# Scaling attention's value result instead of its exponentials in the first six blocks

## The chip, the cores and the metric

The kernel runs on one core of one Trainium2 chip. The metric is device time of one execution in microseconds (us). Before the change the median of three runs was 721.8 us (721.43 to 722.63). A change of less than about 0.2% (1.4 us) cannot be told from none.

## What is computed

Two stages, both in float32, with inputs `q`, `k`, `v` of 4 batches, 8 heads, 768 positions and 64 values per head:

```python
scores = scale * np.matmul(q, k.transpose(0, 1, 3, 2)) + bias      # bias: -slope of the head * distance
scores = np.where(keep, scores, -1e9)                              # 96 positions back, and the first 8
a = np.exp(scores - np.max(scores, axis=-1, keepdims=True))
a = a / (np.sum(a, axis=-1, keepdims=True) + 1e-09)
attn_out = np.matmul(a, v)
x = attn_out.transpose(0, 2, 1, 3).reshape(B * S, H * D)           # 3072 x 512
h = x @ w_in                                                       # 512 x 2048
out = (h * (1.0 / (1.0 + np.exp(-h)))) @ w_out                     # 2048 x 512
```

The weights `w_in` and `w_out` arrive as 64-bit floats, so the kernel first makes float32 of them.

## The kernel before, in words

Attention works in 24 blocks of 128 positions (4 batches of 6), all 8 heads at once, in four pairs of heads (`hp`). For a head, a block's 128 rows of queries meet a window of 232 keys (96 before the block, 8 global ones, the block's own 128); the first block of a batch has 128 keys alone. For each pair:

- TensorE makes the scores (`scores`, L532, for blocks 0 to 5; `stack_scores`, L508, from block 6 on).
- VectorE adds the bias and takes the row's extreme in one instruction (`top_of`, L542), and ScalarE makes the exponentials and their row sums (`expo`, L550).
- VectorE adds 1e-9 to the sums (`guard`, L557), inverts them (`inverse`, L561) and multiplies the exponentials by them, one instruction for each head (`norm`, L566).
- TensorE transposes the scaled exponentials with an identity (`turn_p`, L580), ScalarE copies them out of PSUM (`move_p`, L594).

Then `values_of` (L608) makes the block's result `av` in one bank of PSUM, transposed: its rows are a pair's 2 x 64 values, its columns the 128 positions, for four pairs side by side. ScalarE rounds it to the high part `xh` (L620), and VectorE takes the rest as the low part `xl` (L623).

The second stage works in 12 groups of two blocks (256 positions). For each of 16 chunks `f` of the 2048 inner values: 12 matmuls of L726 (the three products high*high, low*high, high*low of a split float32, 4 row chunks), tanh and the gate (L732 to L744), 6 matmuls of L751 into the group's output banks.

Weights are 32 transfers of 512 KB (`stage`, L364), `w_in` chunk and `w_out` chunk in turn. VectorE makes float32 of a pair of words in three steps (L368, L374, L380), ScalarE rounds it to the high part (L387), VectorE takes the low part (L391). The landing places are three tiles of a pool with the tag "big", and, in turn for two of every five of the first 20 transfers, two places that are filled with weights of their own only at the end ("lent", `wl`).

The order of all this is made beforehand: `Plan.run` walks through a list of operations with a cost, a rank, dependencies and the buffers that they hold, and for every engine takes the lowest rank among the ready ones; the emitted program has that order on each engine, and each engine follows it strictly. While TensorE finds nothing in the first 60 us of the plan, the plan puts in a `filler`, a bf16 matmul on a tile of zeros (L862). Attention's operations have ranks by block and pair, the conversion of transfer `n` has rank 14 + n. So the pairs of blocks 0 to 3 go ahead of most of the conversion, and those of blocks 4 and 5 stand among it.

Of the kernel before, what the change touches and what calls it, by code (L numbers as in the profile page):

```python
# [170 lines left out]
def attn_moe(ctx, tc, q, k, v, n_global, n_local, w_in, w_out, out):  # L171
# [428 lines left out]
    def values(i, hp, av):  # L600
# [3 lines left out]
        for c in range(0 if i % NJ else 1, 2):  # L604
            for a in range(2):
# [5 lines left out]
                )  # L611

    def x_part(i, x):
        g, jj = divmod(i, NB)
# [4 lines left out]
    def x_high(i):
        nc.scalar.copy(x_part(i, "xh"), blk[i]["av"])  # L620

    def x_low(i):
        nc.vector.tensor_sub(x_part(i, "xl"), blk[i]["av"], x_part(i, "xh").bitcast(F32))  # L623
# [414 lines left out]
```

## Time and profile before

| | |
|---|---|
| median of three runs | 721.8 us |
| the profiled execution | 722.34 us |
| its span, first to last instruction | 720.5 us |
| granted TensorE clock, mean | 0.998 |
| busy share: TensorE, VectorE, ScalarE, GpSimd | 98%, 66%, 58%, 3% |

A page of the profile names the engines PE (TensorE matmul), PEld (its weight load), DVE (VectorE), ACT (ScalarE), POOL (GpSimd), SP (SyncE, which issues transfers). Matmuls are pipelined: the duration of one is longer than the step from its start to the next one's start, so a busy PE need not be at its peak. VectorE and ScalarE overlap the end of one instruction with the start of the next by about 0.08 to 0.1 us; in a row of instructions the step from start to start is what one costs. A float32 matmul that is not split stands as two records.

### The profile page before, as it was taken

The numbers are of one execution on the slowest core, as the hardware profiler recorded it, in microseconds if no ns is written. First come the engines' busy times: TensorE is split into PE (matmuls) and PEld (weight loads), VectorE is DVE, ScalarE is ACT, GpSimd is POOL, SyncE is SP. The second block draws the span as 40 slices with busy tenths as digits, with TensorE's granted clock in tenths as the row PEclk, the third lists the DMA queues.
The fourth block names the chain that finished last, engine by engine and source line by source line (L and its number), as shares of the span: only waits on it lengthen the run. The fifth ranks groups of instructions, "written<-read, shape, count | busy, mean of one in ns | idle before, by whom it ended". The sixth has DMA issues, their size and how long they took to land.

```text
span 720.5 us, 14013 instructions
## 1 busy us (share of the span) xinstructions
PE 709.5 (98%) x5144; PEld 630.3 (87%) x5144; DVE 476.1 (66%) x1489; ACT 419.9 (58%) x1097; POOL 24.9 (3%) x81
## 2 busy tenths in 40 slices
PE   8999999999999999999999999999999999999996
PEld 5778899888899999998999999999899999998995
DVE  5999999768756656666566666665665766543332
ACT  5977444579656657566566565665665756443321
POOL 2000000010000000000000000000000000000000
PEclk9999999999999999999999999999999999999999
DMA  8895546362404215124133142340421412000000
GB/s 155 207 246 170 167 126 178 84 173 74 115 12 133 65 51 144 45 71 114 37 97 99 47 116 65 81 112 10 126 73 42 130 30 56 30 2 1 30 1 34
DMA packets 117499, 63.95 MB, mean 89 GB/s; under 512 B 93744, under 2 KB 110384, under 8 KB 117424
## 3 DMA queue, kind: packets, MB, share of 16 engines
q1 hardware_dynamic: 116992, 62.86, 32.3%
q8 instruction: 42, 0.69, 0.4%
q14 instruction: 33, 0.27, 0.1%
q10 hardware_dynamic: 432, 0.13, 0.1%
HBM read 56.69 MB, written 6.29 MB: 87 GB/s over the span
## 4 chain that ended last, share of the span: by engine, by line
PE 92%; ACT 3%; DVE 2%; DMA 1%; issue 1%; SPq 0%; ACTq 0%; DVEq 0%
PE bank L726 36%; PE bank L751 35%; PE bank L608 6%; PE bank L580 5%; PE bank L508 4%; PE bank L448 3%; PE bank L532 2%; ACT pe L550 1%; PE bank L862 1%; DMA c<-in_moe_w_in_dram 1%; DMA qn<-in_q_dram 1%; ACT R L499 0%; DVE th L736 0%; ACT gh L740 0%; DVE pe L542 0%
## 5 line engine op out<-in xcount | busy, mean ns | idle before, releaser
L726 PE MATMUL bank<-xh,WIH 128*128 128x256 f32 x768 | 225.4, 293 | 0.0
L726 PE MATMUL bank<-xl,WIH 128*128 128x256 f32 x768 | 216.2, 281 | 0.0
L726 PE MATMUL bank<-xh,WIL 128*128 128x256 f32 x768 | 215.0, 280 | 0.0
L726 PEld LDWEIGHTS bank<-xh,WIH 128*128 128x128 f32 x768 | 144.7, 188 | 10.3 <-issue 3.3
L726 PEld LDWEIGHTS bank<-xl,WIH 128*128 128x128 f32 x768 | 144.7, 188 | 6.2
L726 PEld LDWEIGHTS bank<-xh,WIL 128*128 128x128 f32 x768 | 144.8, 189 | 0.0
L732 ACT ACTIVATE th<-bank 128x256 f32<-128x256 f32 x192 | 73.7, 384 | 106.1 <-PE bank L726 103.9
L751 PE MATMUL bank<-WOH,gh 128*128 128x512 f32 x336 | 135.2, 403 | 0.0
L751 PE MATMUL bank<-WOH,gl 128*128 128x512 f32 x336 | 132.5, 394 | 0.0
L751 PE MATMUL bank<-WOL,gh 128*128 128x512 f32 x336 | 132.1, 393 | 0.0
L740 ACT CAST gh<-th 128x256 fp32r<-128x256 f32 x192 | 77.2, 402 | 77.3 <-PE bank L751 50.5
L744 DVE TENSOR_TENSOR gl<-th,gh 128x256 fp32r<-128x256 f32 x192 | 81.4, 424 | 54.3 <-ACT gh L740 51.4
L736 DVE SCALAR_TENSOR_TENSOR th<-th,bank 128x256 f32<-128x256 f32 x192 | 80.2, 418 | 55.6 <-ACT th L732 53.5
L550 ACT ACTIVATE pe<-pe,NM 128x232 f32<-128x232 f32 (+1 forms) x192 | 90.7, 473 | 32.0 <-DVE NM L542 30.2
L542 DVE CUSTOM_DVE_ANT_0 pe<-bank,B 128x232 f32<-128x232 f32 (+1 forms) x192 | 68.7, 375 | 55.9 <-PE bank L508 53.0
L751 PEld LDWEIGHTS bank<-WOH,gl 128*128 128x128 f32 x336 | 63.0, 187 | 15.3
L751 PEld LDWEIGHTS bank<-WOH,gh 128*128 128x128 f32 x336 | 63.4, 189 | 7.2 <-issue 0.8
L751 PEld LDWEIGHTS bank<-WOL,gh 128*128 128x128 f32 x336 | 63.4, 189 | 6.8
L594 ACT COPY pt<-bank 128x512 f32<-128x512 f32 (+1 forms) x80 | 43.7, 548 | 28.7 <-PE bank L580 28.5
L566 DVE TENSOR_SCALAR pe<-pe,rs 128x232 f32<-128x232 f32 (+1 forms) x192 | 55.8, 328 | 1.5
L580 PE MATMUL bank<-ident,pe 128*128 128x128 f32 (+1 forms) x352 | 55.7, 275 | 1.1 <-DVE pe L566 1.0
L580 PEld LDWEIGHTS bank<-ident,pe 128*128 128x128 f32 (+1 forms) x352 | 41.4, 136 | 11.3 <-DVE pe L566 2.9
(117 smaller groups left out, 877.7 us busy)
## 6 DMA issues: line engine op xcount, KB each, us to landing
c<-in_moe_w_in_dram SPq DMA_DIRECT2D x16, 512.0 KB, 4.7
c<-in_moe_w_out_dram SPq DMA_DIRECT2D x16, 512.0 KB, 4.4
vn<-in_v_dram SPq DMA_DIRECT2D x24, 256.0 KB, 3.5
w<-in_moe_w_in_dram SPq DMA_DIRECT2D x12, 512.0 KB
w<-in_moe_w_out_dram SPq DMA_DIRECT2D x12, 512.0 KB, 3.7
kn<-in_k_dram SPq DMA_DIRECT2D x23, 256.0 KB, 3.1
qn<-in_q_dram SPq DMA_DIRECT2D x23, 256.0 KB, 3.1
out_dram<-osb SPq DMA_DIRECT2D x23, 256.0 KB, 3.1
```

Of the source, the lines that this page charges most:

```text
L542: nc.vector.tensor_tensor_reduce(t["p", hp][:, a, :n], t["s", hp][a][:, :n], B1[:, h] if i % NJ else B0[:, h], -SC, 3.0e38, ALU.add, ALU.m ...
L550: nc.scalar.activation(x, x, AF.Exp, bias=NM[:, i * H + h:i * H + h + 1], scale=-1.0, accum_out=t["sum", hp][:, a:a + 1],)
L566: nc.vector.tensor_scalar(x, x, t["inv", hp][:, a:a + 1], None, ALU.mult)
L580: nc.tensor.transpose(ps[:n, c, a], pe[:, a, c0:c0 + n], ident)
L594: nc.scalar.copy(t["pt", hp][:, c], t["tp", hp][:, c])
L608: nc.tensor.matmul(pav[r, hp], x[:, 2 * hp + a], pt[:P if c else C1, c, a], start=not c or not i % NJ, stop=c == 1,)
L726: nc.tensor.matmul(ph, w[:, c, fs], x[:, c], start=not c and not n, stop=c == NCC - 1 and n == 2)
L732: nc.scalar.activation(th, mo["ph", g, f], AF.Tanh, scale=0.5)
L736: nc.vector.scalar_tensor_tensor(gf, gf, 1.0, mo["ph", g, f], ALU.add, ALU.mult)
L740: nc.scalar.copy(gh, mo["th", g, f])
L744: nc.vector.tensor_sub(gl, mo["th", g, f], mo["gh", g, f].bitcast(F32))
L751: nc.tensor.matmul(po, a[:, s], w_o(w, f), start=f == 0 and n == 0, stop=f == NFC - 1 and n == 2)
```

## The change

In blocks 0 to 5 the exponentials stay unscaled. The row sums of a block's 8 heads go to one tile of 8 columns (`sums`). When the block's last exponentials are done, VectorE adds 1e-9 (`guard_all`), inverts (`inverse_all`), and writes the rounded inverses and what rounding left to columns 0 to 7 and 8 to 15 of a tile `inv` (`inverse_high`, `inverse_low`). TensorE turns that tile (`turn_inv`), ScalarE copies it out (`move_inv`), and four matmuls with a selecting matrix of zeros and ones (`spread_inv`) write to a bank, for each pair, the inverse sums in the layout of `av`: each of the 64 rows of a head holds that head's inverse of the position. ScalarE copies `av` to SBUF (`move_av`), VectorE multiplies it with the bank (`norm_all`), and `x_high` and `x_low` read the product from SBUF.

GpSimd makes the selecting matrix at the start (`sel`: two clears, 16 selects on 64 columns each, one copy). `inv`, the turned tile and the selecting matrix live in one of the three "big" tiles, held from the start until the last `spread_inv` of block 5. Blocks 6 to 23 are as before. The plan makes its order anew, with all of this in its list.

```diff
+            elif not hp:
+                t["sums"] = x = sb3.tile([P, H], F32, name="sums")
+                for y in range(NHP):
+                    t["sum", y] = x[:, 2 * y:2 * y + 2]
...
+    def sel():
+        nc.gpsimd.memset(st["sel0"], 0.0)
+        for hp in range(NHP):
+            for a in range(2):
+                for p in range(2):
+                    nc.gpsimd.affine_select(
+                        st["sel0"][:, hp, a * D:(a + 1) * D], st["sel0"][:, hp, a * D:(a + 1) * D],
+                        [[0, D]], ALU.not_equal, 1.0, base=-(2 * hp + a + p * H), channel_multiplier=1,
+                    )
+        nc.gpsimd.tensor_copy(st["sel"], st["sel0"])
+    def guard_all(i):
+        x = blk[i]["sums"]
+        nc.vector.tensor_scalar(x, x, 1e-9, None, ALU.add)
+    def inverse_all(i):
+        x = blk[i]["sums"]
+        nc.vector.reciprocal(x, x)
+    def inverse_high(i):
+        nc.vector.tensor_copy(st["inv"][:, :H], blk[i]["sums"])
+    def inverse_low(i):
+        nc.vector.tensor_sub(st["inv"][:, H:2 * H], blk[i]["sums"], st["inv"][:, :H].bitcast(F32))
+    def turn_inv(i, tp):
+        st["it", i] = ps = bank(tp, P)
+        nc.tensor.transpose(ps, st["inv"].bitcast(F32), ident)
+    def move_inv(i):
+        nc.scalar.copy(st["invt"], st["it", i])
+    def spread_inv(i, tp):
+        st["is", i] = ps = bank(tp, NHP, P)
+        for hp in range(NHP):
+            nc.tensor.matmul(ps[:, hp], st["sel"][:, hp], st["invt"], start=True, stop=True)
+    def move_av(i):
+        t = blk[i]
+        t["xq"] = x = sb2.tile([P, NHP, P], F32, name="xq", tag="mid", bufs=5)
+        nc.scalar.copy(x, t["av"])
+    def norm_all(i):
+        t = blk[i]
+        x = t["xq"]
+        nc.vector.tensor_mul(x, x, st["is", i])
+        t["av"] = x
...
+        x = sb3.tile([P, 8, P], F32R, name="inv", tag="big")
...
+    o_sel = op("POOL", 6000, -50, clear, [o_i], [ib, Buf("pt")])
...
-            o = op("DVE", 67, u - PAR["RI"], (lambda i=i, hp=hp: guard(i, hp)), o_e, [pe])
-            o = op("DVE", 72, u - PAR["RI"], (lambda i=i, hp=hp: inverse(i, hp)), [o], [pe])
-            o = [op("DVE", 250 if j else 196, u - PAR["RN"], (lambda i=i, hp=hp, a=a: norm(i, hp, a)), [o], [pe])
-                 for a in range(2)]
+            plain = i >= PAR["IV"]
+            o, o_all = o_e, o_all + o_e
+            if plain:
...
+        if not plain:
+            xq, tp, tq = Buf("pt"), Buf("tp"), Buf("tp")
...
+            m = op("ACT", 478, r, (lambda i=i: move_av(i)), [last], [pav, xq])
+            last = op("DVE", 602, r, (lambda i=i: norm_all(i)), [o, m], [tq, xq, xb[g]["xh"], xb[g]["xl"]])
+            pav = xq
```

How the order moves, at three places. First VectorE (DVE) around the end of block 0. `ISA pe,NM<-...` is `top_of`; before:

```order
L542 ISA pe,NM<-bank_87,B_91 128x128
L542 ISA NM 128x1
L566 TENSOR_SCALAR pe<-pe,rs 128x128 x2
L557 TENSOR_SCALAR rs<-sm 128x2
L542 ISA pe,NM<-bank_85,B_91 128x128
L542 ISA NM 128x1
L561 RECIPROCAL rs<-rs 128x2
L566 TENSOR_SCALAR pe<-pe,rs 128x128 x2
L542 ISA pe,NM<-bank_89,B_90 128x232
```

and now (lines of the new kernel: L547 is `top_of`, L636 to L646 the four steps on the sums, L668 `norm_all`):

```order
L636 TENSOR_SCALAR sums<-sums 128x8
L640 RECIPROCAL sums<-sums 128x8
L547 ISA pe,NM<-bank_87,B_90 128x232
L547 ISA NM 128x1
L643 CAST inv<-sums 128x8
L547 ISA pe,NM<-bank_85,B_90 128x232
L547 ISA NM 128x1
L646 TENSOR_TENSOR inv<-sums,inv 128x8
L547 ISA pe,NM<-bank_88,B_90 128x232
```

Two scalings, a guard and an inverse for each pair are gone; four steps on 8 columns stand once for the block, and `top_of` of the next block moves up between them. Over the program VectorE loses 40 scalings of 232 columns, 8 of 128, 24 guards and 24 inverses, and gains 6 times four small steps and one multiply of 512 columns.

Second, ScalarE (ACT) ahead of its first rounding of weights (L387 `CAST WIH`). Before:

```order
L594 COPY pt<-bank_85 128x512
L550 ACTIVATE pe,sm<-pe,NM 128x232
L511 COPY KHw<-bank_84 128x4x128
L550 ACTIVATE pe,sm<-pe,NM 128x232 x2
L511 COPY QHw<-bank_83 128x512
L550 ACTIVATE pe,sm<-pe,NM 128x232
L594 COPY pt<-bank_88 128x512
L550 ACTIVATE pe,sm<-pe,NM 128x232 x3
L387 CAST WIH<-wf_434 128x4x128
```

and now (L555 is `expo`, L599 `move_p`, L678 `x_high`):

```order
L599 COPY pt_q<-bank_83 128x512
L678 CAST xh<-xq 128x4x128
L555 ACTIVATE pe,sums<-pe,NM 128x232
L599 COPY pt_k<-bank_87 128x512
L555 ACTIVATE pe,sums<-pe,NM 128x232 x2
L599 COPY pt_k<-bank_85 128x512
L511 COPY KHw<-bank_89 128x4x128
L511 COPY QHw<-bank_88 128x512
L599 COPY pt<-bank_84 128x512
L555 ACTIVATE pe,sums<-pe,NM 128x232 x2
L387 CAST WIH<-wf_534 128x4x128
```

The first rounding of weights now stands behind the `xh` of block 1 and several exponentials of later blocks, where before it stood ahead of both.

Third, TensorE (PE) between the value products of block 5 (`pt_k`) and the second stage's group of blocks 4 and 5. Before:

```order
L608 MATMUL bank_85<-pt_k,vp 64x128 x2
L608 MATMUL bank_85<-pt_k,vn 64x128 x2
L751 MATMUL bank_83<-w_last_1780,gh 128x512
L751 MATMUL bank_83<-w_last_1781,gh 128x512
L751 MATMUL bank_83<-w_last_1780,gl 128x512
L448 MATMUL bank_87<-ident,kn 128x128 x4
L751 MATMUL bank_82<-w_last_1780,gh 128x512
L751 MATMUL bank_82<-w_last_1781,gh 128x512
```

(and four more of L751 behind these), and now, with L658 `spread_inv` and L812 the first product of the group:

```order
L613 MATMUL bank_89<-pt_k,vp 64x128 x2
L613 MATMUL bank_89<-pt_k,vn 64x128 x2
L658 MATMUL bank_82<-inv 128x128 x4
L448 MATMUL bank_85<-ident,kn 128x128 x4
L448 MATMUL bank_86<-ident,qn 128x128 x4
L812 MATMUL bank_88<-xh,WIH 128x256
```

Nine products of the second stage that stood between the two have moved ahead of them. Of fillers there were 54 and are 41.

More of the change, by code (lines that the diff above doesn't have):

```diff
@@ L35 @@
     C0=14, CR=1, LW=1, LB=5, QB=3.5, RI=0.1, RN=0, RP=0.2, RM=0, RV=1.2, RQ=0.1, RB=3, LK=-25, LAG=1,
-    BP=(4, 3), NX=20, CF=2, AHEAD=5, CN=4, I0=6, QS='ACT',
+    BP=(4, 3), NX=20, CF=2, AHEAD=5, CN=4, I0=6, IV=6, QS='ACT',
 )
@@ L537, in top_of @@
             t["p", hp] = sb3.tile([P, 2, WIN], F32, name="pe")
-            t["sum", hp] = sb3.tile([P, 2], F32, name="sm")
-            t["inv", hp] = sb3.tile([P, 2], F32, name="rs")
+            if i >= PAR["IV"]:
+                t["sum", hp] = sb3.tile([P, 2], F32, name="sm")
+                t["inv", hp] = sb3.tile([P, 2], F32, name="rs")
+            elif not hp:
+                t["sums"] = x = sb3.tile([P, H], F32, name="sums")
+                for y in range(NHP):
+                    t["sum", y] = x[:, 2 * y:2 * y + 2]
         h, n = 2 * hp + a, cols(i)[1]
@@ L623, in x_low, with clear @@
         nc.vector.tensor_sub(x_part(i, "xl"), blk[i]["av"], x_part(i, "xh").bitcast(F32))
+    ib = Buf("big")
+    def clear():
+        x = sb3.tile([P, 8, P], F32R, name="inv", tag="big")
+        st["inv"], st["invt"], st["sel"] = x[:, 0], x[:, 1], x[:, 2:6]
+        st["sel0"] = sb2.tile([P, NHP, P], F32, name="sel0", tag="mid", bufs=5)
+        nc.gpsimd.memset(x[:, 0].bitcast(F32), 0.0)
+        sel()
+    o_sel = op("POOL", 6000, -50, clear, [o_i], [ib, Buf("pt")])
     kb = [{x: Buf(x) for x in ("KH", "KL", "QH", "QL", "vn", "vp")} | {"R": Buf("big")} for _ in range(B * NJ)]
@@ L681, in attn_moe @@
         pav = Buf("av")
-        last, o_m, pts = None, [], []
+        last, o_m, pts, o_all = None, [], [], []
         for hp in range(NHP):
@@ L713, in attn_moe @@
                 o_m, pts = [], []
+        if not plain:
+            xq, tp, tq = Buf("pt"), Buf("tp"), Buf("tp")
+            r = u - PAR["RI"]
+            o = op("DVE", 67, r, (lambda i=i: guard_all(i)), o_all)
+            o = op("DVE", 72, r, (lambda i=i: inverse_all(i)), [o])
+            o = op("DVE", 72, r, (lambda i=i: inverse_high(i)), [o, before.get("inv"), o_sel], [ib])
+            o = op("DVE", 72, r, (lambda i=i: inverse_low(i)), [o], [ib])
+            o = op("PE", 110, r, (lambda i=i, tp=tp: turn_inv(i, tp)), [o], [tp, ib])
+            o = op("ACT", 160, r, (lambda i=i: move_inv(i)), [o, before.get("invt")], [tp, ib])
+            before["inv"] = o
+            o = op("PE", 440, r, (lambda i=i, tp=tq: spread_inv(i, tp)), [o], [tq, ib])
+            before["invt"] = o
+            m = op("ACT", 478, r, (lambda i=i: move_av(i)), [last], [pav, xq])
+            last = op("DVE", 602, r, (lambda i=i: norm_all(i)), [o, m], [tq, xq, xb[g]["xh"], xb[g]["xl"]])
+            pav = xq
         hi = op("ACT", 478, u, (lambda i=i: x_high(i)), [last], [pav, xb[g]["xh"]])
```

4 lines of the change are left out of this document (added).

## The prediction

> **What bounds the kernel now.** I read the page first, then the busy times by stretch, the chain of waits, and the timelines of VectorE, ScalarE and TensorE at the places that the chain led to.
>
> ```profile
> span 720.5 us, 14013 instructions
> PE 709.5 (98%) x5144; PEld 630.3 (87%) x5144; DVE 476.1 (66%) x1489; ACT 419.9 (58%) x1097; POOL 24.9 (3%) x81
> ```
>
> TensorE is busy for 98%, and VectorE, from which the change takes work, for 66%. Over the whole, VectorE is cover. By stretch it is not (after the stretch: its length, then busy us and instructions of PE, PEld, DVE, ACT, POOL):
>
> ```profile
> 15.00:45.00 30.00, 29.77 (x260) 21.82 (x260) 28.76 (x130) 27.08 (x87) 2.15 (x6) 1.00 0.86 219
> 45.00:75.00 30.00, 30.00 (x228) 25.20 (x229) 30.00 (x105) 21.06 (x60) 0.00 (x0) 1.00 0.64 184
> 75.00:130.00 55.00, 55.00 (x349) 49.52 (x348) 54.83 (x117) 26.20 (x59) 0.00 (x0) 1.00 0.54 162
> L862 PE MATMUL bank<-wx x54: 269/273/421, 1.1 to 50.8; 128*128 128x256 bf16 x54
> ```
>
> ```profile
> 84.75 1.42 PE bank L726 x12
> 90.36 1.42 PE bank L726 x12
> 83.75 0.69 DVE L391 TENSOR_TENSOR WIL<-wf,WIH 128x512 fp32r<-128x512 f32 x1
> 88.77 0.68 DVE L391 TENSOR_TENSOR WIL<-wf,WIH 128x512 fp32r<-128x512 f32 x1
> 134.47 0.68 DVE L391 TENSOR_TENSOR WIL<-wf,WIH 128x512 fp32r<-128x512 f32 x1
> ```
>
> From 45 to 130 us VectorE has no gap (84.83 of 85 us), and from 15 to 45 ScalarE (27.08) is nearly as full as VectorE (28.76). TensorE's busy time there holds fillers, the last at 50.8. The chain shows the coupling: the low part of a `w_in` chunk ends at 84.44 and 89.45, and the 12 matmuls that use it start at 84.75 and 90.36. So until the last `w_in` chunk (134.47) TensorE follows VectorE's conversion; behind it TensorE has a fixed amount of work and sets the end. **The question is by how much that chunk comes earlier, and what is added behind it.**
>
> **The change part by part.** Steps of VectorE and ScalarE, from one start to the next:
>
> ```profile
> 17.54 0.48 DVE L566 TENSOR_SCALAR pe<-pe,rs 128x128 f32<-128x128 f32 x2
> 17.94 0.39 DVE L542 CUSTOM_DVE_ANT_0 pe<-bank,B 128x232 f32<-128x232 f32 x1
> 24.78 0.59 DVE L566 TENSOR_SCALAR pe<-pe,rs 128x232 f32<-128x232 f32 x2
> 25.29 0.39 DVE L542 CUSTOM_DVE_ANT_0 pe<-bank,B 128x232 f32<-128x232 f32 x1
> 25.67 0.17 DVE L557 TENSOR_SCALAR rs<-sm 128x2 f32<-128x2 f32 x1
> 25.75 0.39 DVE L542 CUSTOM_DVE_ANT_0 pe<-bank,B 128x232 f32<-128x232 f32 x1
> 26.07 0.16 DVE L561 RECIPROCAL rs<-rs 128x2 f32<-128x2 f32 x1
> 26.14 0.41 DVE L368 TENSOR_SCALAR wf<-w 128x512 uint32<-128x512 uint32 x1
> 30.38 0.68 DVE L623 TENSOR_TENSOR xl<-bank,xh 128x512 fp32r<-128x512 f32 x1
> 30.98 0.58 DVE L566 TENSOR_SCALAR pe<-pe,rs 128x232 f32<-128x232 f32 x2
> ```
>
> 1. *VectorE's work.* Two scalings of 232 columns take 0.51 us, two of 128 take 0.40, a guard 0.08, an inverse 0.07. Removed: 40 x 0.25 + 8 x 0.20 + 24 x 0.15 = 15.2 us. Added, per block: four small steps, 0.08 each like the guard, and `norm_all`, 512 columns with one operand in PSUM like `xl`, 0.60; 6 x 0.92 = 5.5. Net -9.7 us. In the new order about 3.2 us more has gone behind the last `w_in` low part: both `norm_all` of blocks 4 and 5 (1.2), block 5's four small steps (0.3), two `top_of` of 0.32 (0.6), and some gates of the second stage, a third of a us each. Together **-12.9 us** there, if VectorE keeps as few gaps as now. Its bounds: -9.7 (nothing gained by the order) and -12.9.
>
> 2. *ScalarE before 45 us.*
>
> ```profile
> 25.07 0.48 ACT L550 ACTIVATE pe<-pe,NM 128x232 f32<-128x232 f32 x1
> 25.45 0.19 ACT L550 ACTIVATION_READ_ACCUMULATOR pe<-pe,NM 128x1 f32 x1
> 25.54 0.57 ACT L511 COPY QHw<-bank 128x512 f32<-128x512 f32 x1
> 26.00 0.49 ACT L550 ACTIVATE pe<-pe,NM 128x232 f32<-128x232 f32 x1
> 29.12 0.62 ACT L387 CAST WIH<-wf 128x512 fp32r<-128x512 f32 x1 [0.60 <-DVE wf L380]
> ```
>
> An exponential steps by 0.47 to 0.48, a copy of 512 columns by 0.46 to 0.48. Added per block: `move_av` (0.48) and `move_inv` (128 columns; between nothing and 0.48, I take 0.17, the 512's step in proportion with a fixed part), 0.65; four blocks before 45 us make 2.6 us where 2.9 were free. More weighs the order: counted at these steps, ScalarE has 18.6 us of work ahead of its first rounding of weights before and 26.7 now, since attention comes first. It started that rounding at 29.12, so 10.5 us were idle; with the same idle time it starts at 37.2, where VectorE's own sum (19.2 us ahead of the low part now, 10.4 us idle as now) would want it done by 29.6. VectorE does the steps of later chunks meanwhile, but by the fifth low part ScalarE has 37.5 us to do, 48.0 with the idle time, and VectorE 31.9, 42.8. There VectorE waits 5 us; by the tenth the two sums meet (both at 62.5), and the lag, once VectorE has it, stays, as it has no gap to take it back. Bounds: 1 (exponentials that come sooner without guard, inverse and scaling ahead of them use ScalarE's early idle time) and 5; I take **+4**, nearer to the count.
>
> 3. *The landing places.* `inv` holds one of three "big" tiles up to block 5's end.
>
> ```profile
> 103.75 0.68 DVE L380 SCALAR_TENSOR_TENSOR wf<-w,wf 128x512 uint32<-128x512 uint32 x1
> 104.46 0.33 SPq L364 DMA_DIRECT2D w<-in_moe_w_out_dram  x1
> 109.97 0.42 DVE L368 TENSOR_SCALAR wf<-w 128x512 uint32<-128x512 uint32 x1
> 111.97 0.69 DVE L380 SCALAR_TENSOR_TENSOR wf<-w,wf 128x512 uint32<-128x512 uint32 x1
> DMA to landing us min/median/max: 3.6/3.7/6.7
> c<-in_moe_w_in_dram SPq DMA_DIRECT2D x16, 512.0 KB, 4.7
> ```
>
> A transfer is issued (104.46) when the third step of three transfers earlier ends (104.43), lands in 3.7 us (the fifth row, of tile `w`), and waits until VectorE comes to it at 109.97: 1.8 us of slack. From the first step to the end of the third, 2.7 us pass here. With two tiles a transfer's period is (3.7 + 0.1 + 2.5) / 2 = 3.15 us, 2.5 being between the bare steps (1.6) and this one; VectorE's own work per transfer is about 3.0 in the new order. For the eleven last transfers, which have no lent place, **+1.7**. Bounds: 0 and, at a landing of 4.7 as the later transfers of the same size have it (last row), (4.8 + 2.5) / 2 = 3.65, +7.
>
> 4. *TensorE's work.* 6 transposes and 24 products of 128 columns. What falls before the last `w_in` chunk lies in the waits that end there. Behind it come block 5's spread and turn (0.5 us at 0.11 each), a pair's scores and transposes (0.7), and one more set of L751: three products of 0.23. **+1.9.**
>
> 5. *The handover to blocks 4 and 5.*
>
> ```profile
> 144.58 0.39 PE L608 MATMUL bank<-pt_k,vn 128*64 128x128 f32 x4
> 145.02 0.59 ACT L620 CAST xh<-bank 128x512 fp32r<-128x512 f32 x1 [1.03 <-PE bank L608]
> 145.64 0.69 DVE L623 TENSOR_TENSOR xl<-bank,xh 128x512 fp32r<-128x512 f32 x1 [1.19 <-ACT xh L620]
> 145.70 0.60 PE L448 MATMUL bank<-ident,kn 128*128 128x128 f32 x4
> 146.06 0.71 PE L751 MATMUL bank<-w_last,gh 128*128 128x512 f32 x2
> 147.53 0.28 PE L726 MATMUL bank<-xh,WIH 128*128 128x256 f32 x1
> ```
>
> From the end of the values (144.97) to that of `xl` (146.33) pass 1.4 us, and TensorE has other work to 147.53. Now `move_av` (0.62 with its hop) and `norm_all` (0.72) come between: 2.7 us, and the cover that the order leaves is four spread products and eight transposes, 12 x 0.11 = 1.3. **+1.4**; bounds 0 and 2.7.
>
> The selecting matrix is made on GpSimd before 10 us; block 1's copies on GpSimd wait behind it, and the 232-column scores that need them start at 15 us, so I cost it at nothing (about 1 us if it lasted to 16).
>
> Sum: -12.9 + 4 + 1.7 + 1.9 + 1.4 = **-3.9 us**. Against the profiled execution's 722.3 that is 718.4; against the median of 721.8, 0.5 lower, **717.9 us**.
>
> **The rivals.** (a) *VectorE's whole saving arrives*: ScalarE takes its early idle time (+1), and transfers land in time (0): -12.9 + 1 + 1.9 + 1.4 = -8.6, 713.2 us. For it: ScalarE's 10.5 us idle lie in the start, where exponentials wait for VectorE. Against: 27.08 of 30 us busy right behind it.
>
> (b) *GpSimd holds VectorE at the start; nothing is left.*
>
> ```profile
> 1.51 0.29 DVE L259 TENSOR_TENSOR t<-t,t 128x128 f32<-128x128 f32 x1
> 1.55 0.40 POOL masks.py:199 TENSOR_SCALAR_AFFINE_SELECT ident<-ident 128x128 f32<-128x128 f32 x1
> ```
>
> 16 selects on half of this width, 0.2 to 0.4 us each, run on GpSimd from 2 to between 6 and 9 us, beside the ten VectorE steps that make the bias (5.3 to 7.7 us) and on which the first `top_of` waits. If each of these waited for a select, the start would be 2 to 4 us later: -3.9 + 3.5, about 721.4 us. Here VectorE's L259, with two inputs in SBUF, took 0.29 us beside a select, so the row speaks against it, though VectorE had started first. [...]
>
> (c) *Slower: two landing places are too few.* At the landing of 4.7 us in term 3 the sum is -3.9 + 5.3 = +1.4, and with ScalarE's lag at its 5 it is +2.4: 724.2 us. It decides from a landing of about 4.4 us on (+0.35 us for each of eleven transfers). For it: the 6.7 at most, and the 4.7 of the other 512 KB transfers; against: the median of 3.7 with other loads beside.
>
> **How the numbers follow.** Chances: forecast (715 to 720.2) 0.58, (a) 0.16, (b) 0.13, (c) 0.13. The likeliest gives 717.9 us. Its own range is 715 to 720.2; for 8 in 10 it reaches down to (a), 712.8, and up past (b), 721.8. Faster by over 0.2% (below 720.4, about what a measurement tells from no change): forecast and (a), 0.74; within 0.2%: (b), 0.13; slower: (c), 0.13.
>
> **What would show it.** The last `w_in` low part (L391 before) near 127 us instead of 134.5; near 123 is (a), above 131 is (b) or (c). ScalarE's first rounding of weights at 36 to 37 us, and VectorE waiting for ScalarE between 30 and 50 us. Idle time of VectorE in front of conversion steps, ended by a transfer, of about 0.15 us each after 90 us; more is (c). A wait of TensorE of 1 to 2 us before the group of blocks 4 and 5. The first `top_of` at 8.3 us as now; 10 or later is (b). Wrong would be the reading as a whole if the last low part came 7 us earlier and the end did not follow.

## The result, and the profile after

The changed kernel takes 727.8 us (median; 727.2 to 728.3) where the kernel before took 722.2 (721.4 to 722.8) beside it: a ratio of **1.0076, 95% interval 1.0064 to 1.0088**, 5.5 us slower. The profiled execution's span grew from 720.5 to 726.5 us.

The page of the changed kernel, span and busy time by engine:

```profile
span 726.5 us, 13999 instructions
PE 714.5 (98%) x5161; PEld 635.4 (87%) x5161; DVE 469.6 (65%) x1423; ACT 423.0 (58%) x1109; POOL 30.0 (4%) x100
```

VectorE has lost 6.5 us, TensorE gained 5.0. By stretch, in the columns of the table in the prediction:

```profile
15.00:45.00 30.00, 29.99 (x264) 22.36 (x262) 21.27 (x84) 28.36 (x90) 1.98 (x6) 1.00 0.79 194
45.00:75.00 30.00, 30.00 (x227) 25.24 (x225) 29.92 (x85) 21.96 (x62) 0.00 (x0) 1.00 0.72 208
75.00:130.00 55.00, 55.00 (x350) 49.30 (x349) 51.80 (x110) 24.68 (x58) 0.00 (x0) 1.00 0.52 153
```

From 15 to 45 us VectorE now has 8.7 us without work (1.2 before); the removed work turned into waiting. VectorE's waits there (what waited, for what; total us, times, longest):

```profile
DVE pe L547 <- PE bank L532: 4.1, 4, 3.1
DVE pe L547 <- ACT xq L663: 2.6, 1, 2.6
DVE xq L668 <- ACT KHw L511: 2.5, 1, 2.5
```

The next scores aren't there yet (L532), and ScalarE is full (28.36 of 30 us). The conversions that VectorE could do stand behind these instructions in its queue.

TensorE, from 45 to 130 us, is full before and after. The view that the prediction did not read is TensorE's own waits. These are all of them in the kernel **before**, from 0 to 150 us:

```profile
PE bank L862 <- DVE wx L307: 1.1, 1, 1.1
PE bank L448 <- DMA qn<-in_q_dram: 1.0, 1, 1.0
PE bank L448 <- DMA kn<-in_k_dram: 0.6, 1, 0.6
PE bank L862 <- ACT pt L594: 0.2, 1, 0.2
```

Fillers, and the first q and k. None is on a low part (L391), and from 45 to 150 us the view has no row for either kernel. The starts at 84.75 and 90.36 that the prediction read as coupling come from the chain of waits, and from 78 to 96 us all twelve pieces of that chain are TensorE's own. TensorE's timeline **before**, around the first of them (extract):

```profile
84.36 0.39 PE L751 MATMUL bank<-WOH,gl 128*128 128x512 f32 x1
84.59 0.28 PE L726 MATMUL bank<-xh,WIH 128*128 128x256 f32 x1
84.83 0.28 PE L726 MATMUL bank<-xh,WIL 128*128 128x256 f32 x1
```

The first of the twelve products starts 0.23 us after the last L751 started, which is the usual step of L751. The low part (`WIL`), done at 84.44, is read by the third product only, at 84.83. Nor do the modelled ends of the matmuls hide a wait: from 50.8 to 140.0 us the 348 products of L726 step by 0.120 us on average and the 167 of L751 by 0.237, where the medians over the whole program are 0.118 and 0.233; that is 1.5 us in all. Idle time that could be won lies ahead of that, in the waits above and in the 54 fillers (9.3 us of TensorE's time; 41 and 7.7 us after the change).

The last `w_in` low part of the changed kernel, on VectorE, and the next low part behind it:

```profile
135.77 0.69 DVE L391 TENSOR_TENSOR WIL<-wf,WIH 128x512 fp32r<-128x512 f32 x1
139.48 0.69 DVE L391 TENSOR_TENSOR w_last<-wf,w_last 128x512 fp32r<-128x512 f32 x1 [0.29 <-ACT w_last L387]
```

135.8 instead of 134.5 us, not 127. The new wait is ahead of the group of blocks 4 and 5. Extracts of the timelines there (start, us, engine, line, operation; in brackets the idle time before it and what ended it), TensorE first:

```profile
151.56 0.60 PE L448 MATMUL bank<-ident,qn 128*128 128x128 f32 x4
153.68 0.38 PE L812 MATMUL bank<-xh,WIH 128*128 128x256 f32 x1 [1.51 <-ACT xh L678]
155.25 0.39 PE L812 MATMUL bank<-xl,WIH 128*128 128x256 f32 x1 [1.20 <-DVE xl L681]
```

VectorE:

```profile
151.37 0.69 DVE L668 TENSOR_TENSOR xq<-xq,bank 128x512 f32<-128x512 f32 x1 [2.57 <-ACT xq L663]
153.07 0.68 DVE L495 TENSOR_TENSOR KH<-bank,KH 64x512 fp32r<-64x512 f32 x1 [1.01 <-ACT KL L484]
153.78 0.69 DVE L495 TENSOR_TENSOR KL<-bank,KL 64x512 fp32r<-64x512 f32 x1
154.50 0.69 DVE L681 TENSOR_TENSOR xl<-xq,xh 128x512 fp32r<-128x512 f32 x1
```

ScalarE:

```profile
150.72 0.59 ACT L663 COPY xq<-bank 128x512 f32<-128x512 f32 x1 [1.32 <-PE bank L613]
151.81 0.58 ACT L484 CAST KH<-bank 64x512 fp32r<-64x512 f32 x1 [0.50 <-PE bank L448]
152.40 0.58 ACT L484 CAST KL<-bank 64x512 fp32r<-64x512 f32 x1
153.00 0.62 ACT L678 CAST xh<-xq 128x512 fp32r<-128x512 f32 x1
```

From the values' end (150.67) to that of `xl` (155.19) pass 4.5 us. `norm_all` is done at 152.06, but block 6's copies of k (L484 on ScalarE, L495 on VectorE) stand ahead of `xh` and of `xl`.

To see where time is lost along the way I count TensorE's products of the first stage in the trace, twelve to a set, 192 sets. Start of three sets in us:

| | set 32 | set 33 | set 61 |
|---|---|---|---|
| before | 140.0 | 147.5 | 252.6 |
| after | 141.7 | 153.7 | 258.9 |

The changed kernel is 1.7 us late by 140 us, 4.5 us more by set 33, behind the handover, and hardly any more after it. Not all of the 4.5 is waiting. TensorE stands still for 1.5 us of it (the wait for `xh`); block 5's own turn and spread products take 0.5, and 2.3 is work that the new order moved there: a pair's scores and transposes (1.0), three products of L837 (0.6) and four more turns of block 6 (0.7). The wait for `xl` (1.2) lies behind the start of set 33.

### The profile page after: what moved, and what is told of

The parts are those of the page before. It is cut to its first block, busy times and chain, and to the rows that moved or that the text cites. A ratio compares the mean times of both kernels' runs of the same rounds, so it can differ in the third digit from the quotient of the medians.

```text
span 726.5 us, 13999 instructions
## 1 busy us (share of the span) xinstructions
PE 714.5 (98%) x5161; PEld 635.4 (87%) x5161; DVE 469.6 (65%) x1423; ACT 423.0 (58%) x1109; POOL 30.0 (4%) x100
## 4 chain that ended last, share of the span: by engine, by line
PE 96%; DMA 1%; DVE 1%; ACT 0%; issue 0%; SPq 0%; DVEq 0%; ACTq 0%
PE bank L812 38%; PE bank L837 36%; PE bank L613 6%; PE bank L585 6%; PE bank L508 4%; PE bank L448 3%; PE bank L532 2%; PE bank L948 1%; DMA c<-in_moe_w_in_dram 1%; DMA qn<-in_q_dram 1%; PE bank L658 0%; DVE R L495 0%; PE bank L650 0%; ACT osb L847 0%; DVE th L822 0%
## 5 line engine op out<-in xcount | busy, mean ns | idle before, releaser
L812 PE MATMUL bank<-xh,WIH 128*128 128x256 f32 x768 | 226.4, 295 | 1.5 <-ACT xh L678 1.5
L812 PE MATMUL bank<-xl,WIH 128*128 128x256 f32 x768 | 216.8, 282 | 1.2 <-DVE xl L681 1.2
L812 PE MATMUL bank<-xh,WIL 128*128 128x256 f32 x768 | 215.5, 281 | 0.0
L812 PEld LDWEIGHTS bank<-xh,WIH 128*128 128x128 f32 x768 | 145.0, 189 | 12.4 <-issue 3.6
L812 PEld LDWEIGHTS bank<-xl,WIH 128*128 128x128 f32 x768 | 145.2, 189 | 7.4 <-DVE xl L681 1.4
L812 PEld LDWEIGHTS bank<-xh,WIL 128*128 128x128 f32 x768 | 145.4, 189 | 0.0
L837 PE MATMUL bank<-WOH,gh 128*128 128x512 f32 x336 | 134.8, 401 | 0.0
L837 PE MATMUL bank<-WOH,gl 128*128 128x512 f32 x336 | 132.5, 394 | 0.0
L837 PE MATMUL bank<-WOL,gh 128*128 128x512 f32 x336 | 132.2, 393 | 0.0
L555 ACT ACTIVATE pe<-pe,NM 128x232 f32<-128x232 f32 (+1 forms) x192 | 90.6, 474 | 32.6 <-DVE NM L547 31.1
L547 DVE CUSTOM_DVE_ANT_0 pe<-bank,B 128x232 f32<-128x232 f32 (+1 forms) x192 | 68.6, 376 | 62.2 <-PE bank L508 53.2
L837 PEld LDWEIGHTS bank<-WOH,gl 128*128 128x128 f32 x336 | 63.0, 188 | 15.2
L837 PEld LDWEIGHTS bank<-WOH,gh 128*128 128x128 f32 x336 | 63.3, 188 | 7.4 <-issue 0.5
L837 PEld LDWEIGHTS bank<-WOL,gh 128*128 128x128 f32 x336 | 63.3, 188 | 7.3
L599 ACT COPY pt<-bank 128x512 f32<-128x512 f32 (+1 forms) x80 | 44.0, 550 | 28.1 <-PE bank L585 28.0
L411 DVE TENSOR_REDUCE TOP<-c 128x1 f32<-128x512 int16 x64 | 42.9, 682 | 12.8 <-DMA c<-in_moe_w_in_dram 12.6
## 6 DMA issues: line engine op xcount, KB each, us to landing
vn<-in_v_dram SPq DMA_DIRECT2D x24, 256.0 KB, 4.7
kn<-in_k_dram SPq DMA_DIRECT2D x23, 256.0 KB, 3.0
qn<-in_q_dram SPq DMA_DIRECT2D x23, 256.0 KB, 3.0
out_dram<-osb SPq DMA_DIRECT2D x23, 256.0 KB, 3.1
```

Of the source, the lines that this page charges most:

```text
L411: nc.vector.tensor_reduce(TOP[:, i, n:n + 1], top, AX.X, (ALU.min, ALU.max)[i], apply_absolute_value=True)
L547: nc.vector.tensor_tensor_reduce(t["p", hp][:, a, :n], t["s", hp][a][:, :n], B1[:, h] if i % NJ else B0[:, h], -SC, 3.0e38, ALU.add, ALU.m ...
L555: nc.scalar.activation(x, x, AF.Exp, bias=NM[:, i * H + h:i * H + h + 1], scale=-1.0, accum_out=t["sum", hp][:, a:a + 1],)
L599: nc.scalar.copy(t["pt", hp][:, c], t["tp", hp][:, c])
L812: nc.tensor.matmul(ph, w[:, c, fs], x[:, c], start=not c and not n, stop=c == NCC - 1 and n == 2)
L837: nc.tensor.matmul(po, a[:, s], w_o(w, f), start=f == 0 and n == 0, stop=f == NFC - 1 and n == 2)
```

## The experiments

Two theories stood against each other in the expectations. **V** is the prediction's: TensorE follows VectorE's conversions. **T**: TensorE is bound by its own work, and the loss is made by its added products and the handover. Line numbers of the profiles are those of each kernel. All ratios are to the kernel before, run beside. Us differences are that ratio's distance from 1, times 722. "The head" is the first 45 us. The low part is given by its end, 135.2 before and 136.5 after the change.

| run | ratio, 95% interval | us | last `w_in` low part, end | set 32 | set 33 | set 61 |
|---|---|---|---|---|---|---|
| e1 kept order: before, no scaling | 1.0013, 0.9999 to 1.0028 | +0.9 | 134.9 | 139.8 | 147.4 | 252.5 |
| e1 new order: before, no scaling | 0.9984, 0.9969 to 0.9999 | -1.2 | 127.5 | 140.7 | 146.6 | 250.5 |
| e2: change in blocks 0 to 4 only | 1.0014, 1.0001 to 1.0027 | +1.0 | 134.2 | 140.9 | 149.4 | 255.0 |
| e3: before, products added | 1.0064, 1.0044 to 1.0085 | +4.6 | 137.6 | 143.1 | 151.2 | 256.3 |
| e4: changed, lent places | 1.0048, 1.0032 to 1.0065 | +3.5 | 130.2 | 140.1 | 151.0 | 256.5 |
| e5: changed, block 5's chain first | 1.0052, 1.0033 to 1.0071 | +3.8 | 136.1 | 141.3 | 152.4 | 257.7 |
| e6: changed, gap filled | 1.0069, 1.0052 to 1.0086 | +5.0 | 136.4 | 141.6 | 154.4 | 258.6 |
| e7: before, ScalarE copies added | 1.0045, 1.0028 to 1.0062 | +3.2 | 138.6 | 143.4 | 151.0 | 256.0 |
| e8: changed, no added products | 1.0066, 1.0053 to 1.0080 | +4.8 | 135.3 | 140.5 | 151.9 | 256.9 |
| e9: e4 and e5 together | 1.0044, 1.0030 to 1.0058 | +3.2 | 129.8 | 139.7 | 150.6 | 255.7 |
| e10: e2 with lent places | 0.9993, 0.9984 to 1.0002 | -0.5 | 133.1 | 139.6 | 147.2 | 252.7 |
| e11: before, a big tile held | 1.0030, 1.0018 to 1.0043 | +2.2 | 139.4 | 141.3 | 150.4 | 255.4 |
| e12: e10, copies moved to VectorE | 1.0005, 0.9994 to 1.0015 | +0.4 | 134.2 | 141.0 | 148.7 | 254.1 |
| e13: e2, copies moved, new order | 0.9997, 0.9986 to 1.0008 | -0.2 | 131.3 | 139.1 | 146.8 | 252.2 |
| e14: before, lent places | 1.0002, 0.9991 to 1.0013 | +0.1 | 135.2 | 140.2 | 147.6 | 253.2 |
| e15: e9, copies moved to VectorE | 1.0059, 1.0041 to 1.0078 | +4.3 | 130.9 | 140.8 | 151.7 | 257.0 |

The sets come from one profiled execution each. At set 32, e5 and e6, whose order is the changed kernel's up to block 5, differ from it by up to 0.4 us (141.3 and 141.6, 141.7), and 29 runs of the kernel before, those beside e14, lay between 719.0 and 723.5 us. From these I estimate that differences under about 1 us in these columns say nothing. Where the order was made anew, work also moves from one side of a set to the other.

### e1: VectorE's saving alone

Kept order: three functions of the kernel before return at once.

```diff
 def guard(i, hp):            # inverse and norm likewise
+    if i < 6:
+        return
```

> The kernel before, whose guard, inverse and scaling of blocks 0 to 5 are left out (88 + 8 instructions, 15.2 us of VectorE by the rows of the kernel before); nothing is put in their place, so the exponentials stay unscaled there, and every other instruction stands where it stood. Theory V (the prediction's reading: TensorE follows VectorE's conversions up to the last chunk of w_in): the last low part of w_in near 122 to 125 us instead of 134.5, and the end 9 to 13 us earlier, 709 to 713 us. Theory T (TensorE is bound by its own work from 45 us on; its idle time between 45 and 150 us is all that can be won, and it is small): the last low part comes earlier as much, but the end moves by 0 to 3 us, 719 to 722 us, and TensorE's busy share of 45 to 130 us stays 1.00.

New order: the same steps are left out where the order is made.

```diff
-            o = op("DVE", 67, u - PAR["RI"], (lambda ...: guard(i, hp)), o_e, [pe])
-            ... inverse, norm
+            o = o_e
+            if i >= PAR["I0"]:
+                o = op("DVE", 67, ..., guard ...), inverse, norm as before
```

> The same work left out of the kernel before (guard, inverse and scaling of blocks 0 to 5, exponentials unscaled), but the order is made anew without these steps. Theory V: as with the kept order or better, 708 to 712 us. Theory T: 718 to 722 us; if the order's gain matters it shows as a difference between the two runs of at most 2 us.

Kept order, by stretch:

```profile
15.00:45.00 30.00, 29.77 (x262) 21.95 (x261) 20.87 (x77) 27.48 (x87) 3.12 (x6) 1.00 0.92 219
45.00:75.00 30.00, 30.00 (x230) 25.20 (x230) 25.67 (x71) 20.89 (x59) 0.00 (x0) 1.00 0.61 182
```

Its two largest waits of VectorE from 15 to 75 us:

```profile
DVE pe L542 <- PE bank L586: 4.9, 3, 2.6
DVE th L742 <- ACT th L738: 4.0, 6, 1.3
```

VectorE's busy time falls by 12.2 us in these 60 us (58.76 before, 46.54 here), all of it becomes waiting, and the conversions don't move. The time: +0.9 us (-0.1 to +2.0). That alone would leave V a way out, since the low part didn't come earlier. The new order closes it. The last `w_in` low part on VectorE there, and the stretch ahead of it:

```profile
126.80 0.68 DVE L391 TENSOR_TENSOR WIL<-wf,WIH 128x512 fp32r<-128x512 f32 x1
```

```profile
75.00:130.00 55.00, 55.00 (x356) 49.88 (x355) 54.67 (x117) 26.41 (x59) 0.00 (x0) 1.00 0.49 151
```

The last `w_in` low part starts 7.7 us earlier than before, TensorE is full as ever, set 32 does not come earlier (140.7, with one more block's values, 1.9 us, ahead of it), and the end follows by 1.2 us (0.1 to 2.2). V falls. In these two orders the whole of VectorE's 15.2 us is worth at most some 2 us.

### e3 and e7: what is added, alone, in the order of before

```diff
 def values_of(i, av):        # e3
+    for _ in range(5 if i < 6 else 0):
+        nc.tensor.matmul(bank(av, 2 * P), warm[:, :P], warm, start=True, stop=True)
```

> The kernel before with TensorE's added products alone: five products of 256 columns in bf16 (0.11 us each, as the fillers) ahead of the values of each of the blocks 0 to 5, 30 in all, 3.3 us; every other instruction stands where it stood and VectorE's work is unchanged. Theory V (the prediction's term 4: what falls before the last chunk of w_in lies in waits): block 5's alone count, +0.5 us, 722 to 722.7 us. Theory T (TensorE full by its own work): they are added at their price, less what lies ahead of 45 us in place of waits: +2 to +3.3 us, 724 to 725.5 us.

+4.6 us (3.2 to 6.1) for 3.3 us of products; set 32 is 3.1 us late already. Products ahead of the last chunk count in full, as T says and against the prediction's term 4.

```diff
 def x_high(i):               # e7
-    nc.scalar.copy(x_part(i, "xh"), blk[i]["av"])
+    for _ in range(3 if i < 4 else 1):
+        nc.scalar.copy(x_part(i, "xh"), blk[i]["av"])
```

> The kernel before, in whose blocks 0 to 3 the copy of the high part (512 columns, 0.46 to 0.48 us on ScalarE) is made three times: 8 copies, 3.8 us more of ScalarE's time before 45 us, where the change adds 2.6; all else stands as it stood. By the prediction's term 2 (ScalarE's lag ahead of 45 us reaches the end at 1 to 5 us for 2.6): +2 to +5 us, 724 to 727 us. Theory T in its strict form (only TensorE's own work and the wait at the handover count): 0 to +1 us, 721.5 to 723 us.

+3.2 us (2.0 to 4.5), 0.84 us for each of the 3.8 added. By stretch:

```profile
15.00:45.00 30.00, 27.66 (x247) 20.29 (x245) 26.14 (x119) 27.78 (x84) 2.22 (x6) 1.00 0.80 210
45.00:75.00 30.00, 29.01 (x218) 23.30 (x217) 29.15 (x102) 22.86 (x64) 0.00 (x0) 1.00 0.62 175
```

TensorE gets gaps it did not have, 2.1 us from 15 to 45 and 1.0 behind. So strict T is wrong as well: in the order of before, ScalarE's time in the head reaches the end, as term 2 said.

### e2, e5, e6: the handover

```diff
-    ... I0=6, IV=6, QS='ACT',
+    ... I0=6, IV=5, QS='ACT',          # e2: block 5 as before
```

> The changed kernel with the change in blocks 0 to 4 alone; block 5 is as before. The held big tile is given back when block 4 is done, shortly ahead of block 5, so the landing places stay two during the conversions. If the wait ahead of the group of blocks 4 and 5 (3.3 us of idle TensorE and 1.7 us at half clock behind it in the changed kernel) is a cost of its own: TensorE has no wait of over 1 us at 150 to 156 us, its clock stays 1.00, and the time is 722 to 724 us. By the prediction's terms, which put 1.4 us on this handover and 0.5 on block 5's products: 725.5 to 726.5 us.

+1.0 us: block 5's share of the change is worth 4.5 of the 5.5 us (1.0076 less 1.0014). TensorE has no wait there (5.00 of 5.00 us busy from 150 to 155), and set 33 comes 4.3 us earlier than in the changed kernel. The five products less, and the held tile that is given back before block 5, are in this 4.5 too.

```diff
+    chain = [order[place(f, 5)] for f in ("norm_all", "x_high", "x_low")]     # e5
+    order = [x for x in order if x not in chain]
+    n = max(place("move_av", 5), place("spread_inv", 5)) + 1
+    order[n:n] = chain
```

> The changed kernel, in whose order block 5's scaling, high part and low part stand right behind its move_av and spread products, ahead of block 6's first two copies of k on ScalarE and their low parts on VectorE; no other instruction is moved. If the 3.3 us without work on TensorE at 152 to 155.3 us are made by this chain with block 6's copies in between: the first product of the group starts near 153.5 instead of 155.25, the gap is 1.5 to 2 us, and the time falls by 1.5 to 3.5 us (724 to 726 us; the more, if the half clock behind the gap goes too). If only the number of steps in the chain counts, the copies of block 6 then wait instead and TensorE waits for its scores: 727 to 728 us.

TensorE's waits from 140 to 175 us in this kernel:

```profile
PE bank L508 <- ACT R L499: 0.9, 2, 0.7
PE bank L585 <- DVE pe L571: 0.8, 2, 0.6
PE bank L812 <- ACT xh L678: 0.6, 1, 0.6
PE bank L812 <- DVE xl L681: 0.3, 1, 0.3
```

The wait for `xh` and `xl` shrinks from 2.7 to 0.9 us, and 0.9 comes back as a wait for block 6's `R`: +3.8 us, 1.7 less than the changed kernel, though the intervals of the two touch. The copies of block 6 in between made part of this wait.

```diff
 def moe_h(g, f, c, h):       # e6
+    if g == 2 and f == c == 0:
+        for _ in range(24):
+            filler(h)
```

> The changed kernel with 24 products of 256 columns (0.11 us each, 2.6 us, of no use) right ahead of the first product of the group of blocks 4 and 5, in the gap in which TensorE has no work; all else stands as it stood. If the half clock from 156.4 us on comes of the gap: the granted clock stays 1.00 at 155 to 160 us, and the time falls by 1 to 2 us, 725.5 to 727 us. If the clock is independent of the gap: it falls again and the time is 727.5 to 728.5 us.

The granted clock (third number from a row's end) in the changed kernel, and with the gap filled:

```profile
153.00:156.40 3.40, 1.53 (x10) 1.33 (x11) 3.21 (x5) 2.92 (x5) 1.75 (x4) 1.00 1.11 210
156.40:159.80 3.40, 3.40 (x19) 3.40 (x17) 1.08 (x3) 2.65 (x6) 0.00 (x0) 0.50 0.24 50
```

```profile
153.00:156.40 3.40, 3.05 (x27) 2.70 (x25) 3.27 (x5) 2.82 (x5) 1.75 (x4) 1.00 1.13 214
156.40:159.80 3.40, 3.40 (x29) 3.23 (x28) 0.98 (x3) 2.96 (x6) 0.00 (x0) 1.00 0.40 88
```

The half clock comes of the gap; without it the clock stays at 1.00. But the time, +5.0 us, cannot be told from the changed kernel's +5.5. By set 61 the two are 0.3 us apart: what the half clock costs seems to be taken up by waits that TensorE has behind it anyway. With the gap filled TensorE is busy for 4.41 of the 5 us from 160 to 165, in the changed kernel for 5.00 and before the change for 4.65.

### e4, e9, e11: the landing places

```diff
-    BP=(4, 3), NX=20,
+    BP=(4, 3), NX=25,                  # e4, in the changed kernel
```

> The changed kernel with lent landing places for the transfers 23 and 24 as well (NX=25 in place of 20), so that fewer late transfers depend on the two big tiles that the held tile leaves. By the prediction's term 3 (two places cost 1.7 us, up to 7, on the path): the last low part of w_in 2 to 4 us earlier than the changed kernel's 136.5 us and the end as much, 723 to 726 us. Theory T (TensorE has work of its own until 145 us and isn't held by the transfers): the low part comes earlier, TensorE's idle time up to 145 us stays, and the end moves by less than the low part does, 0 to 1.5 us: 726 to 728 us.

The low part comes 6.3 us earlier than in the changed kernel, the end 2.0 us (3.5 instead of 5.5). The time, 725.3 us, lies in the range given for term 3 and just below T's. But the end does not follow the low part one to one, as term 3 would have it. Set 32 gains 1.5 us and set 33 2.7. From 140 to 175 us TensorE's wait for `xh` is gone, and that for `xl` is 1.7.

> The changed kernel with both remedies: lent places for transfers 23 and 24 (NX=25), and block 5's scaling, high part and low part ahead of block 6's copies. Alone they gave 0.28 and 0.24% against the changed kernel. If they remove the same wait ahead of the group of blocks 4 and 5: 724.5 to 725.5 us; if they add up: 723.2 to 724.5 us. In both cases it stays slower than before by at least 1 us, since the 3 us of products are left.

Both remedies together: +3.2 us, where each alone gave +3.5 and +3.8. They remove the same wait (TensorE waits 0.2 us for `xl` here) and don't add up. The about 3 us that stay are not simply the added products: e10 below keeps 25 of the 30 and loses nothing. TensorE's other waits from 125 to 175 us in e9:

```profile
PE bank L508 <- ACT R L499: 0.9, 2, 0.7
PE bank L585 <- DVE pe L571: 0.9, 2, 0.6
```

They are for block 6. The same view of e10 has no row. With the 0.2 for `xl` these waits make 2.0 of the 3.7 us between the two runs; the rest is open.

```diff
+    o_hold = op("POOL", 200, -50, hold, [o_i], [ib])       # e11, in the kernel before
     ...
+        if i == 5:
+            op("POOL", 100, u, let_go, [last, o_hold], [ib])
```

> The kernel before, in which a big tile of no use is held from the start to the end of block 5's values (written and read once by GpSimd), as inv is in the changed kernel: two landing places for transfers in place of three; the order is made anew with it. By the prediction's term 3 at its value: +1.7 us, 723.9 us, bounds 0 and +7. Theory T: in the changed kernel the places used up what VectorE had gained, so without that gain they cost more, +3 to +6 us, 725 to 728 us, as a wait of TensorE that begins before 145 us.

+2.2 us (1.3 to 3.1), beside term 3's value of 1.7; my own expectation of 3 to 6 fails. Set 33 is 2.9 late. Where on the way it is lost, the sets do not show: the new order moved one block's values (1.9 us) behind set 32.

### e8: the products, in the changed kernel

```diff
 def turn_inv(i, tp):
-    nc.tensor.transpose(ps, st["inv"].bitcast(F32), ident)
 def move_inv(i):
-    nc.scalar.copy(st["invt"], st["it", i])
+    nc.scalar.copy(st["invt"], ident)
 def spread_inv(i, tp):       # its four products go
 def norm_all(i):
-    nc.vector.tensor_mul(x, x, st["is", i])
+    nc.vector.tensor_mul(x, x, x)
```

> The changed kernel without TensorE's added work: the 6 transposes of the inverses and the 24 spread products are left out, move_inv copies the identity instead and norm_all multiplies xq by itself, so the values are not scaled; every other instruction stands where it stood. Theory T (each added product is on the path, 30 x 0.11 = 3.0 us with the transposes): 3 us less than the changed kernel, 724.3 to 725.3 us, with the wait at the handover still there. By the prediction's term 4 (only block 5's 0.5 us count): 726.8 to 727.5 us.

0.7 us less than the changed kernel, not 3 (30 x 0.11 would even be 3.3), and the intervals overlap, so it cannot be told from no gain (by set 61 the one profiled execution is 2.0 us earlier). T's price from e3 does not hold in the changed order. There ScalarE is full. From 15 to 45 us in this kernel, and below it a wait of TensorE behind the handover:

```profile
15.00:45.00 30.00, 29.71 (x256) 21.25 (x256) 21.83 (x89) 29.36 (x93) 2.14 (x6) 1.00 0.83 208
```

```profile
PE bank L585 <- DVE pe L571: 0.9, 2, 0.6
```

ScalarE is busy for 29.36 of 30 us, the waits at the handover stand as they were (1.5 for `xh`, 1.2 for `xl`), and 0.9 us of waiting for `pe` come behind them, which the changed kernel does not have. So part of the products lies in time that TensorE would not have used.

### e10, e12 to e15: can the freed time be used?

e10 is e2 with NX=25.

> The change in blocks 0 to 4 alone, with lent places for transfers 23 and 24 too: the mildest form of the change. Theory T: its 25 products cost 2.5 us, the shorter head gives back 1 to 2: 721.5 to 723.5 us, not faster than before by more than 0.2%. Theory V (VectorE's saving of 12.7 us counts once the places are back and the handover is as before): 712 to 717 us.

-0.5 us (-1.2 to +0.1): the mildest form of the change makes no difference. Its 721.6 us are in T's range; V's was 712 to 717. e12 moves six copies from ScalarE to VectorE in it, in the kept order:

```diff
 def high(i, nm, p0=0, p1=NHP):
+    if 0 < i < 4:
+        nc.vector.tensor_copy(o, x)
+    else:
         nc.scalar.copy(o, x)
```

> The kernel of e10 (change in blocks 0 to 4, lent places for transfers 23 and 24), in which the copies of the turned k and q of blocks 1 to 3 (6 copies of 512 columns, 2.9 us of ScalarE) are made on VectorE (about 0.6 us each), which is idle for 7.5 of the 30 us from 15 to 45; everything stands where it stood. If ScalarE holds the head (0.84 us per us, as the added copies in the kernel before showed): 2 to 2.4 us less than e10, 719 to 719.7 us, faster than before by 0.3 to 0.4%. If VectorE's own wait for these scores, in order, takes its place: 721 to 723 us.

+0.4 us, no better than e10. By stretch, then ScalarE's two largest waits from 15 to 45 us:

```profile
15.00:45.00 30.00, 29.89 (x263) 22.16 (x262) 23.11 (x87) 26.56 (x85) 1.97 (x6) 1.00 0.80 192
```

```profile
ACT pt L603 <- PE bank L589: 1.7, 1, 1.7
ACT pe L559 <- DVE NM L551: 1.3, 4, 0.4
```

ScalarE's busy time falls by 2.6 us (29.14 in e10), and it waits for TensorE's transposes and VectorE's row extremes instead. This fits a head that is held by the chain that passes through all three engines, not by the sum of one of them. The rest says the same: made anew for it (e13) and with the whole change (e15), the moved copies bring nothing, and lent places alone don't move the kernel before (e14).

> The change in blocks 0 to 4 with the copies of k and q of blocks 1 to 3 on VectorE, the order made anew for it, without the added lent places. If ScalarE holds the head: 719 to 721 us. If not: 721.5 to 723 us, as the change in blocks 0 to 4 alone.

> The kernel before with lent places for transfers 23 and 24 (NX=25), nothing else. With three big tiles for transfers a landing has 1.8 us of slack there, so both theories expect no change within 1 us: 721 to 723 us. If it is faster by 1 us or more, the time of the change in blocks 0 to 4 with lent places owes that to the places and not to the change.

> The whole change (blocks 0 to 5) with both remedies (lent places, block 5's chain first) and the copies of k and q of blocks 1 to 3 on VectorE in the kept order. If ScalarE holds the head: 2 to 2.4 us less than with the remedies alone (725.2), 722.8 to 723.2 us, still slower than before by the products. If not: 725 to 726 us.

No version that computes the whole result beats the kernel before by more than its interval allows.

## Why the prediction was wrong, step by step

1. **VectorE's work, -12.9 us: the step that failed.** It rests on "until the last `w_in` chunk (134.47) TensorE follows VectorE's conversion". The evidence was a set of products that starts 0.31 us behind a low part, and an engine that is full. Both are what one sees, too, when two full engines run side by side in an order made to fit, and the chain of waits had no VectorE in it there. TensorE had no wait on VectorE from 45 to 150 us, and was busy for 85.00 of 85 us in the very rows that the prediction quoted. Measured: -1.2 us (e1 new order), nothing in the kept order. The sentence on what would prove the reading wrong came true in e1: the last low part 7.7 us earlier, and the end not behind it.
2. **ScalarE's lag, +4.** In the order of before ScalarE's time in the head has its price (e7: +3.2 us for 3.8 us of copies). In the changed kernel the order was made anew, with the first rounding of weights at 37.15 us (predicted 36 to 37). VectorE's waits for ScalarE from 30 to 50 us came to 2.6 us, not 5 (and by the term's own figures 31.9 and 10.4 make 42.3, not 42.8). Everything added ahead of set 32, products too and less what VectorE's saving gave back, cost 1.7 us (2.7 if the scores and transposes that moved behind it are counted), and relieving ScalarE gained nothing (e12: +0.4 us, beside -0.5 in e10). So the term was probably too large; no run gives its size by itself.
3. **The landing places, +1.7.** About right in size, by luck: 2.2 us in the kernel before (e11), 2.0 in the changed one (e4). Wrong in the working. From transfer 20's low part (100.60 us) to the last one's (140.18), eleven transfers later, one took 3.6 us, where 3.15 was reckoned (before: 106.30 to 137.47, 2.83). But VectorE did not wait for a transfer there. Its waits from 88 to 142 us in the changed kernel, the two largest:

```profile
DVE gl L830 <- ACT gh L826: 1.7, 4, 0.8
DVE xq L668 <- ACT xq L663: 1.4, 1, 1.4
```

   They end on ScalarE; the slower pace probably lies in these and in the order that was made for two places. What the places cost came by way of the handover (e4: TensorE's waits there are 1.7 us in place of 2.7) and the head; how much by which is not shown. The landing that the term used for these places is that of the `w_out` transfers alone: no view gives one for the `w_in` transfers into them.
4. **TensorE's work, +1.9.** "What falls before the last chunk lies in the waits that end there" is wrong: there are no such waits, and e3 paid for every product (+4.6 us for 3.3 us of them). The scores and transposes that it books behind the last chunk did move behind set 32 (1.0 us), but TensorE was spared them ahead of it; the three products of L751 came forward from behind set 33. Work that moves is not added work, and TensorE is full before and after (55.00 of 55 us from 75 to 130 in both). The number is near what e8 shows (0.7 by the times, 2.0 by the trace): that is luck, as the reason, time that TensorE would not have used, was not named for it.
5. **The handover, +1.4.** The right place and the right cover: TensorE's other work ended at 152.16, 1.5 us behind the values. The chain was taken for 2.7 us and took 4.5, as block 6's four copies between its steps were not counted, so TensorE waits 2.7 us (1.5 and 1.2), not 1.4. Block 5's share of the change came to 4.5 us in all (e2), the largest single part of the loss.

With the sizes measured: 1.7 ahead of set 32 (with what VectorE's saving gave back already in it) and 4.5 from there to set 33, 6.2 us, beside 6.0 of the span and 5.5 by the ratio. By the runs: the change in blocks 0 to 4 with enough landing places costs nothing (e10, -0.5), the held place 1.5 more (e2, +1.0; the two intervals just touch), block 5 the other 4.5.

Of the rivals, (a) falls with term 1. (b) falls by its own mark: the first `top_of` starts at 8.24 us (8.26 before), and the sixteen selects took 0.24 us each. One step of VectorE took longer, beside GpSimd's copy of the finished matrix (6.75 to 7.36 us): L285, 0.64 us in place of 0.26. The next two start 0.3 to 0.4 us later, and the idle time ahead of the first `top_of`, 0.56 us before the change, takes that up. The changed kernel's group on GpSimd, and extracts of VectorE's timeline:

```profile
L628 POOL TENSOR_SCALAR_AFFINE_SELECT sel<-sel 128x64 f32<-128x64 f32 x16 | 3.5, 243 | 0.6
```

```profile
6.79 0.64 DVE L285 TENSOR_SCALAR t<-t,par 128x96 f32<-128x96 f32 x1
8.24 0.29 DVE L547 CUSTOM_DVE_ANT_0 pe<-bank,B 128x128 f32<-128x128 f32 x1 [0.24 <-ACT B L298]
```

(c) named the right side for another reason: VectorE's waits from 88 to 142 us have no transfer among them (one of `w_in` issued at 120.44 us was taken up at 124.37, without idle time in front), and the two places made about 2 of the 5.5 us.

## What to carry to other kernels

Before work taken from an engine is booked as a gain, look at the waits of the engine that sets the end: if none of them ends on that engine's work, the gain is at most the idle time of the engine that sets the end, fillers counted as idle, however full the other one is (here 15.2 us of VectorE's work were worth 1.2 us in e1's new order, and nothing in the kept one). A chain that is made longer is priced with everything that stands between its steps in each queue (here 2.7 us reckoned, 4.5 us taken). What an added step costs depends on who is full at that place in that order, so a price measured in the old order (4.6 us for 3.3 us of products in e3, 3.2 us for 3.8 us of copies in e7) need not hold in the new one (0.7 us back in e8 without the products, no gain in e12 with 2.6 us less of ScalarE).

## What was not expected of the hardware

TensorE's clock fell to half after short gaps. In the changed kernel the trace's clock record shows full speed for 139.9 us, half for 3.41, and full again; it fell behind a stretch of 3.4 us in which TensorE was busy for 1.53. In e4 it fell too, behind one wait of 1.74 us, and in e8, with waits of 1.51 and 1.19 us, it did not. e4, then e8, in stretches of 3.4 us:

```profile
151.20:154.60 3.40, 1.66 (x14) 1.51 (x13) 3.15 (x5) 2.42 (x5) 1.48 (x3) 0.99 0.69 189
154.60:158.00 3.40, 3.40 (x19) 3.40 (x17) 0.95 (x3) 3.09 (x6) 0.00 (x0) 0.50 0.59 135
```

```profile
148.50:151.90 3.40, 1.89 (x25) 1.48 (x21) 1.30 (x2) 2.40 (x5) 0.00 (x0) 1.00 0.74 221
151.90:155.30 3.40, 2.21 (x17) 2.00 (x17) 2.84 (x5) 2.49 (x5) 1.75 (x4) 1.00 1.20 211
```

In the clock records of the two kernels the stretches at full clock are whole numbers of 3.413 us: 41 and 165 in the changed kernel (139.95 and 563.20 us), 206 in the kernel before (703.15 us). Counted in such steps, the three that are followed by half clock, one at this gap and one at the end of each program, hold 1.56, 0.38 and 0 us of TensorE's work, the 409 others at least 2.56. The stretch ahead of the fall in e4 holds 1.66 us, the two of e8, where the clock stayed at 1.00, hold 1.89 and 2.21. No run was made to tell whether the work within such a step, the length of a wait or something else makes the clock fall.
